# Attention-then-FFN kernel: token chunks of 112 partitions with the last 16 tokens in the first chunk, split loads, and small-tile matmuls collected into three bundles a batch

## The chip, the cores and the metric

One core of a Trainium2 chip runs the whole program. The metric is device time in microseconds (us) of one execution; three runs of the kernel before gave 705.81, 705.86 and 706.18, median 705.86.

## What is computed

```python
# q, k, v: (8 batches, 8 heads, 576 tokens, 64); phi: (8, 8, 576, 32), float32
a = exp(phi - max(phi, axis=2)); a = a / (sum(a, axis=2) + 1e-9)      # over the tokens
k_m = einsum('bhsm,bhsd->bhmd', a, k); v_m = einsum('bhsm,bhsd->bhmd', a, v)
scores = q @ k_m.T / 8
attn = softmax(scores, axis=-1)                                        # over 32 memories
x = (attn @ v_m) as (4608 tokens, 512)
h = x @ w_in                                                           # w_in: (512, 2048)
out = (h * erf(softplus(h))) @ w_out                                   # w_out: (2048, 512)
```

## The kernel before, in words

The kernel never forms `x`. For each batch it multiplies the 32 memories of each head of `v_m` into `w_in` once (`vw`, L675), so that the first FFN product of a hidden chunk of 128 is attention weights times `vw` (`ffn1`, L752, matmul L770). Matmuls of that stage and of the second FFN product (`ffn2`, L851, matmul L847) are made at float32 accuracy from three fp32r products of a high and a low part. Steps are numbered by (batch, hidden chunk): 16 chunks a batch, 128 steps in all. One step is two halves of `ffn1` (6 matmuls of 288 columns each into a bank of tag `ps`), softplus, erf and a product on ACT and DVE, and 12 matmuls of `ffn2` of an earlier step into four `pso` banks. The 64 tokens of a batch that are left over 4 x 128 go two batches at a time through `ffn2_rest` (L869, tile `psr`, one `ps` bank for its whole run).

**Small-tile work on PE.** Beside these full-array matmuls each batch needs: the sums over tokens that make `k_m` and `v_m` (`sums_and_turn`, L580, matmul L598; 128x32 tiles of the array), their turning by transposes (L629), the transposes that spread the maxima of phi (`phi_numbers`, L508, L515), two groups of score matmuls (`attention`, L700, through `of_heads`, L663, matmul L667, 64x32 tiles) and four groups of `vw` (also L667, 64x32 tiles, 512 columns; 256 columns in batch 0). The transposes use the whole 128x128 array. `together` (L546) makes operations that are to be issued in one run, of kind "small"; `bundle` (L948) and the list `PARTS` (L975 to 992) say at which step which of them go together. For batches 3 to 7 the work for batch b stands in four bundles, all during batch b-1: sums with `vw` 4, turn with phi_numbers of the next batch and `vw` 8, scores 2b with `vw` 12, scores 2b+1 with the first `vw` of batch b. In the last batch three `vw` bundles stand alone.

**Order.** The order on each engine is fixed when the program is built. `Plan` runs a list scheduler over all operations, with a rank for each (`at(step)`), a cost, an engine or two ways, and room in each pool (`room`, L306: four `ps` banks; 4 + 4 tiles of `at_hi` and `at_lo`; five `raw` tiles). L1016 to 1021 shift the ranks of eight operations and fix the engine of one. Each DMA is issued on SP (`load`, L388), at the start also on ACT (`queue`, L384). At the start of the program PE is filled with dummy matmuls (`fill`, L372).

**Loads.** Tokens lie on 116 partitions in five chunks; the host pads each chunk to 128 rows (`rows`, L1049). A `kv` load (`load_kv`, L412) moves 128 partitions x 5 chunks x 1 KB = 640 KB, of which 64 KB is padding rows; q of half a batch is one load of 576 KB into a `raw` tile (`load_q`, L418; into `wo` for batch 0).

Of the kernel before, what the change touches and what calls it, by code (L numbers as in the profile page):

```python
# [32 lines left out]
ROW = 116  # L33
# [214 lines left out]
def tile_memory_attention_then_erf_softplus_ffn(  # L248
# [29 lines left out]
    ROWS = [min(ROW, S - c * ROW) for c in range(NC)]  # L278
    assert NC == -(-S // ROW) and D < ROWS[-1] and H == 8
# [11 lines left out]
        for n, b, kw in (  # L291
# [4 lines left out]
            ("at", 4, {}),  # L296
# [9 lines left out]
    room = {"wo": NPR, "vw_hi": 2, "vw_lo": 2, "at_hi": 4, "at_lo": 4, "h": HB, "e": EB}  # L306
# [111 lines left out]
    def load_q(rank, u, tag="raw"):  # L418
        key = tile_(tag, "q", u, shape=[P, NP_, U], pool=tag)
        b, hf = divmod(u, 2)  # L420
        load(rank, P * NP_ * U * 4, [key], lambda: nc.sync.dma_start(
            out=get(key),
            in_=qT[b, hf].rearrange("r (p s) -> r p s", p=NP_)))


# [82 lines left out]
    def phi_numbers(rank, b):  # L508

        a, bias = ("phi", b), ("bias", b)  # L510
        ps = tile_("ps", "psa", "max", b, shape=[P, H * M], pool="ps")

        def turn():
            for g in range(NG):
                nc.tensor.transpose(  # L515
                    out=get(ps)[:, g * P : (g + 1) * P], in_=get(bias)[:, g], identity=ident
                )

        yield
        yield 2 * 108, [bias], [ps], [], turn  # L520
        op(DVE, on_dve(NC * H * M), rank, [a, ps], [a], lambda: nc.vector.tensor_tensor(  # L521
            out=get(a)[:ROW], in0=get(a)[:ROW],
            in1=get(ps)[:ROW].unsqueeze(1).to_broadcast([ROW, NC, H * M]), op=ALU.add))
        op(ACT, on_act(NC * H * M), rank, [a], [a], lambda: nc.scalar.activation(
            get(a)[:ROW], get(a)[:ROW], AF.Exp), kind="exp")

    def memories(rank, rank_2, b, parts):

        a = ("phi", b)
        phi_sums(rank, b)  # L530
        if b:
            together(rank, phi_numbers(rank, b))
        else:
            tile_("raw", *a, shape=[P, NC, H * M], pool="raw")
            n = NC - 1
            for g in range(NG):
                numbers_of(rank, b, g, range(n), tile_("ps", "psa", "a", g, shape=[P, n, P], pool="ps"), 0)
            last = tile_("ps", "psa", "a", NG, shape=[P, NG, P], pool="ps")
            for g in range(NG):
                numbers_of(rank, b, g, range(n, NC), last, g)  # L540
# [5 lines left out]
    def together(rank, *pieces):  # L546
# [5 lines left out]
        holds = [k for w in works for k in w[2] + w[3]]  # L552
        for n, (cost, _, writes, _, emit) in enumerate(works):
            x = op(PE, cost, rank + n * 1e-3, reads, writes, emit, kind="small",
                   holds=[] if n else holds)
            x.follows, before_it = before_it, x
        for x in pieces:
            next(x, None)

    def numbers_of(rank, b, g, cs, ps, at):  # L560

        t, a, n, ln = ("phiT", b, g), ("phi", b), len(cs), ROWS[cs[0]]

        def turn():
            for c in cs:
                nc.tensor.transpose(
                    out=get(ps)[:ln, at + c - cs[0], :], in_=get(t)[:, c * ROW : c * ROW + ln], identity=ident
                )
# [11 lines left out]
    def sums_and_turn(rank, b, part, rank_2=None):  # L580
# [5 lines left out]
        ps, t = ("psa", "kmvm", b, part), ("kvk", b, part)  # L586
        ps_2 = ("psa", "turn", b, part)
# [4 lines left out]
        def sums():  # L592
            for n, g in enumerate(gs):
                for c, ln in enumerate(ROWS):
                    for j in range(4):
# [3 lines left out]
                            out=get(ps)[M * j : M * (j + 1), n, :w],  # L599
# [8 lines left out]
        def first():  # L608
            tile_("ps", *ps, shape=[P, 4, P], pool="ps")
            tile_("dk", *t, shape=[P, 4, 2, D], pool="att")  # L610
            yield
            yield n_g * NC * 110 * n_x, [a] + kvs, [ps], [t], sums
            for n, g in enumerate(gs):
                rs = ("prs", b, g)

                def keep(f, n=n):
                    return lambda: f(
                        get(t)[:, n * n_x : (n + 1) * n_x],
                        get(ps)[:, n, : n_x * D].rearrange("p (x d) -> p x d", d=D).unsqueeze(2)
                        .to_broadcast([P, n_x, 2, D]))  # L620

                op(ACT, on_act(2 * n_x * D, True), rank, [ps, rs], [(t, n)],
# [40 lines left out]
    def of_heads(ps, w, x):  # L663
        for p in range(NP_):
            for par in range(2):
                rows = slice(par * D, (par + 1) * D)
                nc.tensor.matmul(  # L667
                    out=get(ps[par])[p * M : (p + 1) * M, :],
                    lhsT=w[rows, p, :],
                    rhs=x[rows, p, :],  # L670
# [4 lines left out]
    def vw(rank, b, k, n, exact):  # L675
# [3 lines left out]
        if k % 4 == 0:  # L679
            tile_("vw_hi", *hi, shape=[P, 2, 512], dtype=F32 if exact else F32R, pool="vw")  # L680
            if not exact:
# [5 lines left out]
               lambda: of_heads(ps, vm[b % 2], w_in_sb[i][:, :, cols]))  # L687
# [12 lines left out]
    def attention(rank, rank_2, u):  # L700
        b = u // 2
        s = tile_("sc", "sc", u)
        ps = heads(U, "sc", u)
        yield
        yield (4 * U / 2.4, [("km", b % 2), ("q", u)], ps, [s],
               lambda: of_heads(ps, km[b % 2], get(("q", u))))
# [7 lines left out]
        for g in range(NG):  # L714
            op(DVE, on_dve(U), rank, [ps[g]], [(s, g)], lambda g=g: nc.vector.transpose(
                out=get(s)[:, g, :], in_=get(ps[g])))
# [152 lines left out]
    def ffn2_rest(rank, b, first, n):  # L869
# [12 lines left out]
        op(PE, 3 * n * mm(DM, False), rank, reads + [o], [o], emit)  # L882
# [14 lines left out]
    def at(step):  # L897
        return 100 * step
# [13 lines left out]
    for n, name in enumerate(FIRST):  # L912
# [5 lines left out]
        elif name[:-1] == "q":  # L918
            load_q(rank, x, "wo")
# [33 lines left out]

    for b in range(1, B):
        o = NK * b
        n = o - 12 if b == 1 else o - {2: 18, 3: 26}.get(b, 34)
        for g in range(NG):
            when(n, load_phiT, at(n - 6 if b <= 2 else n - 3), b, g)
        n, n_3 = (n if b <= 3 else o - 28), n + 2
        when(n, load_phi, at(n - 5), b)  # L960
        n_2 = n if b <= 2 else o - 17
# [3 lines left out]
        if b > 2:  # L965
            when(n_3, phi_sums, at(n_3), b)
        else:
            if b == 1:
                when(n, memories, at(n), at(n + 3), b, TOGETHER)
            else:  # L970
                when(n, phi_sums, at(n), b)
        for x in range(2):
            n = o - 8 + 4 * x if b == 1 else o - 13
            when(n, load_q, at(n - 4 + 2 * x), 2 * b + x)
        PARTS = [(o - 8, [(attention, 2 * b)]), (o - 4, [(attention, 2 * b + 1), (vw, b, 0)])]  # L975
        if b > 1:
            m = o - (11 if b == 2 else 15)
            sums, turn = sums_and_turn(at(m), b, TOGETHER[0], at(o - 11))
            PARTS = [(m, [(sums,), (vw, b - 1, 8 if b == 2 else 4)])]
            if b == 2:  # L980
                PARTS = [(o - 15, [(phi_numbers, b), (vw, b - 1, 4)])] + PARTS
            later = [(phi_numbers, b + 1)] if b + 1 < B else []
            PARTS += [
                *([(o - 11, [(turn,)]), (o - 3, later)] if b == 2 else
                  [(o - 11, [(turn,)] + later + [(vw, b - 1, 8)])]),
                (o - 7, [(attention, 2 * b), (vw, b - 1, 12)]),
                (o - 4, [(attention, 2 * b + 1), (vw, b, 0)]),
            ]
        if b == B - 1:
            PARTS += [(o + 1, [(vw, b, 4)]), (o + 5, [(vw, b, 8)]), (o + 9, [(vw, b, 12)])]  # L990
        for n, fs in PARTS:
            when(n, bundle, at(n), fs)
# [93 lines left out]
```

## Time and profile before

| | us |
|---|---|
| median of three runs | 705.86 |
| the profiled execution, its own time | 706.31 |
| its span, first to last instruction | 704.5 |
| PE busy | 696.3 |
| ACT busy | 488.7 |
| DVE busy | 448.9 |
| POOL busy | 108.2 |

The profile has the busy time of each engine, the span in 40 slices, the chain of work that ended last, and groups of instructions by source line. Matmuls are pipelined, so what a matmul costs PE is read from the distance between starts, not from the duration of one. [...]

### The profile page before, as it was taken

What the parts mean: (1) busy time and instruction counts of PE and PEld (TensorE: products, weight loads), DVE (VectorE), ACT (ScalarE), POOL (GpSimd) and SP (SyncE); (2) the same over time, 40 slices, a digit from 0 to 9 for tenths busy, and PEclk for the clock granted to TensorE, in tenths of its full rate; (3) what the DMA queues carried; (4) which work ended last, traced back from release to release, by engine and by line L of the source; (5) the groups of instructions that cost most, each with busy time, mean ns of one, the idle gap of its engine ahead of it and who ended that gap; (6) DMA issues with size and microseconds to landing.
All of it is one profiled execution on the core that took longest, in us unless ns stands there. A gap on an engine that the chain in (4) does not pass through costs nothing.

```text
span 704.5 us, 12292 instructions
## 1 busy us (share of the span) xinstructions
PE 696.3 (99%) x4858; PEld 560.5 (80%) x4858; DVE 448.9 (64%) x774; ACT 488.7 (69%) x793; POOL 108.2 (15%) x262
## 2 busy tenths in 40 slices
PE   8999999999999999999999999999999999999997
PEld 4556588888888888888888788888888888888886
DVE  4999999468734686567734677546764348745530
ACT  4899989757855768787754867776665556776821
POOL 0032135112111111111201111101111011111110
PEclk9999999999999999999999999999999999999999
DMA  9999100712312115030132102311120100010002
GB/s 362 418 414 417 40 26 17 297 41 68 117 65 92 55 38 181 30 102 13 56 150 77 44 27 68 151 60 38 39 68 1 61 15 1 1 60 1 1 1 75
DMA packets 17833, 66.71 MB, mean 95 GB/s; under 512 B 2032, under 2 KB 2032, under 8 KB 17776
## 3 DMA queue, kind: packets, MB, share of 16 engines
q1 hardware_dynamic: 17408, 64.85, 24.8%
q10 hardware_dynamic: 368, 1.08, 0.4%
q8 instruction: 38, 0.62, 0.4%
q14 instruction: 19, 0.16, 0.1%
HBM read 56.49 MB, written 9.44 MB: 94 GB/s over the span
## 4 chain that ended last, share of the span: by engine, by line
PE 92%; DMA 4%; DVE 2%; ACT 1%; issue 0%; SPq 0%
PE pso L847 50%; PE psh L770 28%; PE psr L847 6%; PE psa L667 6%; PE psa L598 2%; DMA q<-qT 2%; DMA phiT<-phiT 2%; PE psa L629 0%; DVE w L441 0%; PE psa L515 0%; DVE phi L521 0%; DVE pmx L490 0%; ACT L810 0%; ACT e L805 0%; DVE sc L729 0%
## 5 line engine op out<-in xcount | busy, mean ns | idle before, releaser
L847 PE MATMUL pso<-wo,g_hi 128*128 128x512 f32 x960 | 300.0, 394 | 0.0
L847 PEld LDWEIGHTS pso<-wo,g_hi 128*128 128x128 f32 x960 | 172.2, 188 | 41.1 <-issue 12.6
L847 PE MATMUL pso<-wo,g_lo 128*128 128x512 f32 x480 | 188.2, 392 | 0.0
L788 ACT ACTIVATE h<-psh 128x288 f32<-128x288 f32 x176 | 71.6, 409 | 137.1 <-PE psh L770 136.7
L836 DVE TENSOR_TENSOR e<-e,h 128x576 f32<-128x576 f32 x120 | 88.6, 754 | 51.2 <-ACT e L810 51.1
L843 POOL CAST rest<-g_hi 128x64 fp32r<-128x64 f32 x120 | 55.0, 458 | 423.4 <-DVE g_hi L838 419.3
L838 DVE CAST g_hi<-e 128x576 fp32r<-128x576 f32 x120 | 53.9, 450 | 101.3 <-PE pso L847 96.7
L770 PE MATMUL psh<-at_hi,vw_hi 128*128 128x288 f32 x496 | 109.5, 302 | 0.0
L847 PEld LDWEIGHTS pso<-wo,g_lo 128*128 128x128 f32 x480 | 90.1, 188 | 20.6
L770 PE MATMUL psh<-at_lo,vw_hi 128*128 128x288 f32 x496 | 106.2, 296 | 0.0
L770 PE MATMUL psh<-at_hi,vw_lo 128*128 128x288 f32 x496 | 105.6, 294 | 0.0
L770 PEld LDWEIGHTS psh<-at_hi,vw_hi 128*128 128x128 f32 x496 | 85.7, 188 | 21.0 <-issue 3.7
L839 DVE TENSOR_TENSOR g_lo<-e,g_hi 128x576 fp32r<-128x576 f32 x120 | 92.3, 769 | 7.6 <-POOL rest L843 0.5
L805 ACT ACTIVATE e<-h 128x576 f32<-128x576 f32 x127 | 86.7, 685 | 3.4 <-DVE h L787 0.7
L810 ACT ACTIVATE e<-e 128x576 f32<-128x576 f32 x128 | 79.8, 675 | 0.4
L770 PEld LDWEIGHTS psh<-at_hi,vw_lo 128*128 128x128 f32 x496 | 79.9, 188 | 0.0
L770 PEld LDWEIGHTS psh<-at_lo,vw_hi 128*128 128x128 f32 x496 | 79.3, 188 | 0.0
L843 POOL CAST rest<-g_lo 128x64 fp32r<-128x64 f32 x120 | 40.7, 340 | 98.8 <-DVE g_lo L839 95.9
L847 PE MATMUL psr<-wo,rest 128*128 128x512 f32 x192 | 49.1, 391 | 0.0
L365 ACT ACTIVATE vw_hi<-psa 128x512 fp32r<-128x512 f32 (+1 forms) x68 | 34.8, 555 | 18.7 <-PE psa L667 18.6
L367 DVE TENSOR_TENSOR vw_lo<-psa,vw_hi 128x512 fp32r<-128x512 f32 (+1 forms) x68 | 40.6, 636 | 9.8 <-ACT vw_hi L365 9.5
L847 PEld LDWEIGHTS psr<-wo,rest 128*128 128x128 f32 x192 | 36.0, 188 | 8.7 <-POOL rest L843 0.8
(81 smaller groups left out, 650.4 us busy)
## 6 DMA issues: line engine op xcount, KB each, us to landing
kv<-kv SPq DMA_DIRECT2D x31, 640.0 KB, 8.1
q<-qT SPq DMA_DIRECT2D x16, 576.0 KB, 5.4
out<-ot SPq DMA_DIRECT2D x32, 256.0 KB, 2.0
w<-w_in SPq DMA_DIRECT2D x8, 1023.8 KB, 15.6
w<-w_out SPq DMA_DIRECT2D x8, 1023.8 KB, 14.8
phi<-phi SPq DMA_DIRECT2D x7, 640.0 KB, 7.1
phiT<-phiT SPq DMA_DIRECT2D x15, 288.0 KB, 3.8
out<-ot SPq DMA_DIRECT2D x7, 128.0 KB, 2.3
```

Of the source, the lines that this page charges most:

```text
L365: lambda: nc.scalar.activation(get_hi(), get_src(), AF.Identity))
L367: lambda: nc.vector.tensor_tensor(out=get_lo(), in0=get_src(), in1=get_hi().bitcast(F32), op=ALU.subtract))
L667: nc.tensor.matmul(out=get(ps[par])[p * M : (p + 1) * M, :], lhsT=w[rows, p, :], rhs=x[rows, p, :], start=True, stop=True,)
L770: nc.tensor.matmul(out=get(ps)[:, :U], lhsT=x[:, g, k % 4 * P : (k % 4 + 1) * P], rhs=y[:, g, :], start=(n + g == 0), stop=(n == len(parts ...
L788: other={ACT: (on_act(U, True), lambda: nc.scalar.activation(keep(), get(ps), AF.Identity))})
L805: last[:] = [op(ACT, on_act(S), rank, [("h", i)], [e], lambda: nc.scalar.activation(get(e), get(("h", i)), AF.Softplus), kind="softplus", ...
L810: last[:] = [op(ACT, on_act(S), rank, [e], [e], lambda: nc.scalar.activation(get(e), get(e), AF.Erf), kind="erf", edge=edge, after=last)]
L836: op(DVE, on_dve(S), rank, [e, h], [e], lambda: nc.vector.tensor_tensor(out=get(e), in0=get(e), in1=get(h), op=ALU.mult))
L838: op(DVE, on_dve(S, 1), rank, [e], [hi], lambda: nc.vector.tensor_copy(out=get(hi), in_=get(e)))
L839: op(DVE, on_dve(S), rank, [e, hi], [lo], lambda: nc.vector.tensor_tensor(out=get(lo), in0=get(e), in1=get(hi).bitcast(F32), op=ALU.subtract))
L843: lambda x=x, y=y: nc.gpsimd.tensor_copy(out=rest[:, k, x, cols], in_=get(y)[:, NT * P :]))
L847: nc.tensor.matmul(out=o, lhsT=y, rhs=z, start=(start and n == 0), stop=(stop and n == len(parts) - 1))
```

## The change

1. **Layout.** `ROW` is 112. The chunks are 128, 112, 112, 112, 112 tokens: the first chunk holds tokens 0 to 111 on partitions 0 to 111 and the last 16 tokens on partitions 112 to 127. The host lays out `kv`, `phi` and `phiT` so. The phi operations cover 128 partitions instead of 116.
2. **Loads.** A `kv` load is two transfers: 112 partitions x 5 KB, and 16 partitions x 1 KB. From batch 1 on, q of half a batch is two transfers of half the size into tiles of the pool `at`, no longer `raw`. `at_hi` and `at_lo` share eight tiles `at` with them.
3. **Bundles.** `PARTS` is rewritten. In batches 2 to 6 it has three bundles: at step 1 scores 2b+2 with `vw` 4; at step 7.5 `vw` 8 with `vw` 12; at step 12 the sums of batch b+2, scores 2b+3 and the first `vw` of batch b+1. The last batch has two. `phi_numbers` and the turn stand alone (`alone`, no longer of kind "small"). From batch 3 on the sums are written into columns 288 to 415 of the two banks of the scores they are bundled with, and not into a bank of their own.
4. **Smaller edits.** The transposes of `phi_numbers` also wait for the phi load. `ffn2_rest` comes two operations a step from step 2, not one a step from step 0, and its first follows the last bundle made. Ten ranks and four engine choices replace the list at L1016.

The core of the diff:

```diff
-ROW = 116
+ROW = 112
-    ROWS = [min(ROW, S - c * ROW) for c in range(NC)]
+    ROWS = [P] + [ROW] * (NC - 1)
-    room = {"wo": NPR, "vw_hi": 2, "vw_lo": 2, "at_hi": 4, "at_lo": 4, "h": HB, "e": EB}
+    room = {"wo": NPR, "vw_hi": 2, "vw_lo": 2, "at": 8, "h": HB, "e": EB}
...
-        load(rank, P * NC * 4 * D * 4, [key], lambda: queue(b, g if x == 0 else 0).dma_start(out=get(key), in_=src))
+        by = queue(b, g if x == 0 else 0)
+        load(rank, ROW * NC * 4 * D * 4, [(key, 0)], lambda: by.dma_start(out=get(key)[:ROW], in_=src[:ROW]))
+        load(rank, (P - ROW) * 4 * D * 4, [(key, 1)],
+             lambda: by.dma_start(out=get(key)[ROW:, 0], in_=src[ROW:, 0]))
...
+        for x in range(2):
+            key = tile_("at", "q", u, x, shape=[P, 2, U], pool="at")
+            load(rank, P * 2 * U * 4, [key], lambda x=x, key=key: nc.sync.dma_start(
+                out=get(key), in_=src[:, 2 * x : 2 * x + 2]))
...
-        yield 2 * 108, [bias], [ps], [], turn
+        yield 2 * 108, [bias, a], [ps], [], turn
...
+        banks = [ps] * n_g if into is None else [("psa", "sc", into, n) for n in range(n_g)]
...
+    def alone(rank, x):
+        together(rank, x, kind=None)
...
-            PARTS = [(m, [(sums,), (vw, b - 1, 8 if b == 2 else 4)])]
...
-                  [(o - 11, [(turn,)] + later + [(vw, b - 1, 8)])]),
-                (o - 7, [(attention, 2 * b), (vw, b - 1, 12)]),
-                (o - 4, [(attention, 2 * b + 1), (vw, b, 0)]),
...
-            PARTS += [(o + 1, [(vw, b, 4)]), (o + 5, [(vw, b, 8)]), (o + 9, [(vw, b, 12)])]
+            PARTS += [
+                (o + 1, [(phi_numbers, 2), (vw, 1, 4)]),
+                (o + 5, [(sums[2],), (vw, 1, 8)]),
+                (o + 5, [(turn[2],)]),
+                (o + 9, [(attention, 4), (vw, 1, 12)]),
+            ]
+        elif b < B - 1:
+            PARTS += [(o + 1, [(attention, 2 * b + 2), (vw, b, 4)]), (o + 7.5, [(vw, b, 8), (vw, b, 12)])]
+        else:
+            PARTS += [(o + 1, [(vw, b, 4)]), (o + 7.5, [(vw, b, 8), (vw, b, 12)])]
+        if b + 2 < B:
+            n = o + 10 if b == 1 else o + 8
+            when(n, lambda n=n, b=b: alone(at(n), phi_numbers(at(n), b + 2)))
+            n = o + 14
+            when(n, lambda n=n, b=b: alone(at(n), turn[b + 2]))
+        if b + 1 < B:
+            PARTS += [(o + 12, with_sums(b + 2) + [
+                (attention, 2 * b + 3, 2 * D * (b + 2 < B)), (vw, b + 1, 0)])]
...
-            n = (b + 1) * NK + k // 2 if b < B - 1 else max(second[NS - NK + k + 1] + 1, NS)
+            n = (b + 1) * NK + 2 + k // 4 if b < B - 1 else max(second[NS - NK + k + 1] + 1, NS)
...
-        90: 380, 128: 213, 179: 257, 222: 139, 250: -309, 251: -309, 252: -309, 253: -309,
+        67: -130, 95: -149, 108: -209, 134: 157, 213: 238, 259: -312, 260: -312, 296: 307,
+        303: 463, 597: 396,
-    for n, e in {105: ACT}.items():
+    for n, e in {109: DVE, 136: ACT, 326: DVE, 500: DVE}.items():
```

## Rows read from the trace of the kernel before

**Rows 1.** The page: busy time, share of the span and instructions of each engine; and by line, the shares of the chain that ended last.

```profile
PE 696.3 (99%) x4858; PEld 560.5 (80%) x4858; DVE 448.9 (64%) x774; ACT 488.7 (69%) x793; POOL 108.2 (15%) x262
PE pso L847 50%; PE psh L770 28%; PE psr L847 6%; PE psa L667 6%; PE psa L598 2%; DMA q<-qT 2%; DMA phiT<-phiT 2%; PE psa L629 0%; DVE w L441 0%; PE psa L515 0%; DVE phi L521 0%; DVE pmx L490 0%; ACT L810 0%; ACT e L805 0%; DVE sc L729 0%
```

**Rows 2.** Windows of the span: stretch, its length, busy us of PE, weight loads, DVE, ACT and POOL (instructions), granted clock, DMA share, GB/s.

```profile
4.00:20.00 16.00, 14.58 (x242) 7.91 (x240) 9.92 (x22) 6.44 (x14) 0.00 (x0) 1.00 1.02 422
20.00:40.00 20.00, 19.46 (x128) 12.66 (x122) 19.74 (x29) 18.48 (x34) 0.56 (x2) 1.00 1.01 415
40.00:70.00 30.00, 29.71 (x247) 18.10 (x246) 29.39 (x43) 29.31 (x49) 9.72 (x13) 1.00 1.02 417
70.00:100.00 30.00, 30.00 (x176) 20.69 (x175) 30.00 (x52) 26.20 (x40) 8.75 (x10) 1.00 0.13 45
100.00:650.00 550.00, 549.63 (x3832) 457.60 (x3831) 342.94 (x606) 385.58 (x625) 82.86 (x214) 1.00 0.19 65
```

**Rows 3.** PE in order of time around one bundle of scores and `vw` (start us, us from first start to last end, line, tiles, shape, count).

```profile
401.50 0.62 PE L847 MATMUL pso<-wo,g_hi 128*128 128x512 f32 x2
401.96 0.40 PE L847 MATMUL pso<-wo,g_lo 128*128 128x512 f32 x1
402.28 0.72 PE L667 MATMUL psa<-q,km 64*32 64x288 f32 x16
402.79 1.06 PE L667 MATMUL psa<-w_in,vm 64*32 64x512 f32 x16
403.79 0.74 PE L847 MATMUL pso<-wo,g_hi 128*128 128x512 f32 x2
404.37 0.39 PE L847 MATMUL pso<-wo,g_lo 128*128 128x512 f32 x1
```

**Rows 4.** PE in order of time: the other small-tile operations of the same batch, then the three of the last batch; between them stand only full-array matmuls.

```profile
348.10 2.40 PE L598 MATMUL psa<-kv,phi 116*32 116x128 f32 x80
350.43 1.09 PE L667 MATMUL psa<-w_in,vm 64*32 64x512 f32 x16
...
393.69 0.60 PE L629 MATMUL psa<-ident,kvk 128*128 128x128 f32 x4
394.12 0.38 PE L515 MATMUL psa<-ident,bias 128*128 128x128 f32 x2
394.44 1.09 PE L667 MATMUL psa<-w_in,vm 64*32 64x512 f32 x16
...
421.36 0.72 PE L667 MATMUL psa<-q,km 64*32 64x288 f32 x16
421.87 1.06 PE L667 MATMUL psa<-w_in,vm 64*32 64x512 f32 x16
...
603.34 1.09 PE L667 MATMUL psa<-w_in,vm 64*32 64x512 f32 x16
...
622.69 1.09 PE L667 MATMUL psa<-w_in,vm 64*32 64x512 f32 x16
...
641.24 1.09 PE L667 MATMUL psa<-w_in,vm 64*32 64x512 f32 x16
```

**Rows 5.** Windows of line L667 alone, 100 to 650 us: PE busy us and matmul records, then the weight loads.

```profile
100.00:650.00 550.00, 35.22 (x624) 8.57 (x624) 1.00 0.19 65
```

**Rows 6.** PE in order of time: a `vw` group of 256 columns early in the program, with what follows it.

```profile
56.71 0.66 PE L667 MATMUL psa<-w_in,vm 64*32 64x256 f32 x16
57.30 0.53 PE L770 MATMUL psh<-at_hi,vw_hi 128*128 128x288 f32 x2
```

**Rows 7.** PE in order of time: transposes followed by full-array matmuls.

```profile
129.16 0.66 PE L629 MATMUL psa<-ident,kvk 128*128 128x128 f32 x4
129.57 0.70 PE L847 MATMUL pso<-wo,g_hi 128*128 128x512 f32 x2
130.11 0.40 PE L847 MATMUL pso<-wo,g_lo 128*128 128x512 f32 x1
```

**Rows 8.** The chain that ended last, its first 30 us in order of time (start us, us, what).

```profile
0.74 3.88 DMA phiT<-phiT
...
4.64 12.99 DMA q<-qT
...
17.76 0.82 PE psa L667 x16
18.58 0.83 DVE sc L715 x2
...
25.29 1.14 DVE w_in L465
```

**Rows 9.** DVE in order of time: the transposes of the second half batch's scores, with the idle time before them.

```profile
18.56 0.85 DVE L715 STREAM_TRANSPOSE sc<-psa 128x288 f32<-128x288 f32 x2 [0.86 <-PE psa L667]
```

**Rows 10.** SP's queue in order of time: the DMA issues of the first 20 us (three of them).

```profile
1.19 0.42 SPq L416 DMA_DIRECT2D kv<-kv  x1
2.60 1.05 SPq L416 DMA_DIRECT2D kv<-kv  x2
4.64 0.33 SPq L421 DMA_DIRECT2D q<-qT  x1
```

**Rows 11.** The page's DMA issues: tile, queue, count, KB each, median us from issue to landing.

```profile
kv<-kv SPq DMA_DIRECT2D x31, 640.0 KB, 8.1
...
phi<-phi SPq DMA_DIRECT2D x7, 640.0 KB, 7.1
...
out<-ot SPq DMA_DIRECT2D x7, 128.0 KB, 2.3
```

**Rows 12.** What ACT and DVE did right after the bundle of rows 3 (start us, us, line, operation, tiles, shapes, count, idle before).

```profile
403.95 1.09 ACT L365 ACTIVATE vw_hi<-psa 128x512 fp32r<-128x512 f32 x2 [0.91 <-PE psa L667]
403.09 0.85 DVE L715 STREAM_TRANSPOSE sc<-psa 128x288 f32<-128x288 f32 x2 [1.62 <-PE psa L667]
403.97 0.75 DVE L718 TENSOR_REDUCE smx<-sc 128x18 f32<-128x576 f32 x1
404.64 1.28 DVE L367 TENSOR_TENSOR vw_lo<-psa,vw_hi 128x512 fp32r<-128x512 f32 x2
```

**Rows 13.** Two of PE's weight loads' waits, whole run: who waited for whom, us in total, times, longest us.

```profile
PEld psa L667 <- issue: 5.9, 23, 0.4
PEld psr L847 <- POOL rest L843: 0.8, 1, 0.8
```

More of the change, by code (lines that the diff above doesn't have):

```diff
@@ L277, in tile_memory_attention_then_erf_softplus_ffn @@
     NC = phi.shape[2]
-    ROWS = [min(ROW, S - c * ROW) for c in range(NC)]
-    assert NC == -(-S // ROW) and D < ROWS[-1] and H == 8
+    ROWS = [P] + [ROW] * (NC - 1)
+    AT = [sum(ROWS[:c]) for c in range(NC)]
+    assert sum(ROWS) == S and D < ROW and H == 8
     RAW = 5
@@ L415, in load_kv, with load_q, q_keys, q_of @@
         src = kv[b - 1, 2 * g + x] if b else kv_0[x, g]
-        load(rank, P * NC * 4 * D * 4, [key], lambda: queue(b, g if x == 0 else 0).dma_start(out=get(key), in_=src))
-    def load_q(rank, u, tag="raw"):
-        key = tile_(tag, "q", u, shape=[P, NP_, U], pool=tag)
-        b, hf = divmod(u, 2)
-        load(rank, P * NP_ * U * 4, [key], lambda: nc.sync.dma_start(
-            out=get(key),
-            in_=qT[b, hf].rearrange("r (p s) -> r p s", p=NP_)))
+        by = queue(b, g if x == 0 else 0)
+        load(rank, ROW * NC * 4 * D * 4, [(key, 0)], lambda: by.dma_start(out=get(key)[:ROW], in_=src[:ROW]))
+        load(rank, (P - ROW) * 4 * D * 4, [(key, 1)],
+             lambda: by.dma_start(out=get(key)[ROW:, 0], in_=src[ROW:, 0]))
+    def load_q(rank, u):
+        b, hf = divmod(u, 2)
+        src = qT[b, hf].rearrange("r (p s) -> r p s", p=NP_)
+        if u < 2:
+            key = tile_("wo", "q", u, shape=[P, NP_, U], pool="wo")
+            load(rank, P * NP_ * U * 4, [key], lambda: nc.sync.dma_start(out=get(key), in_=src))
+            return
+        for x in range(2):
+            key = tile_("at", "q", u, x, shape=[P, 2, U], pool="at")
+            load(rank, P * 2 * U * 4, [key], lambda x=x, key=key: nc.sync.dma_start(
+                out=get(key), in_=src[:, 2 * x : 2 * x + 2]))
+    def q_keys(u):
+        return [("q", u)] if u < 2 else [("q", u, x) for x in range(2)]
+    def q_of(u, rows, p):
+        return get(("q", u))[rows, p] if u < 2 else get(("q", u, p // 2))[rows, p % 2]
     wo, wf, raw_of = {}, {}, {}
@@ L536, in memories @@
             for g in range(NG):
-                numbers_of(rank, b, g, range(n), tile_("ps", "psa", "a", g, shape=[P, n, P], pool="ps"), 0)
-            last = tile_("ps", "psa", "a", NG, shape=[P, NG, P], pool="ps")
+                numbers_of(rank, b, g, range(1, NC), tile_("ps", "psa", "a", g, shape=[P, n, P], pool="ps"), 0)
+            whole = tile_("ps", "psa", "a", NG, shape=[P, NG, P], pool="ps")
             for g in range(NG):
-                numbers_of(rank, b, g, range(n, NC), last, g)
+                numbers_of(rank, b, g, range(1), whole, g)
         for turn_n, part in enumerate(parts):
@@ L544, in memories, with together @@
             together(rank_2 + turn_n * 0.01, second)
-    def together(rank, *pieces):
+    bundles = []
+    def together(rank, *pieces, kind="small"):
         for x in pieces:
@@ L551, in together @@
         reads = [k for w in works for k in w[1]]
-        holds = [k for w in works for k in w[2] + w[3]]
+        holds = [k[0] if isinstance(k[0], tuple) else k for w in works for k in w[2] + w[3]]
         for n, (cost, _, writes, _, emit) in enumerate(works):
-            x = op(PE, cost, rank + n * 1e-3, reads, writes, emit, kind="small",
+            x = op(PE, cost, rank + n * 1e-3, reads, writes, emit, kind=kind,
                    holds=[] if n else holds)
             x.follows, before_it = before_it, x
+        if kind == "small":
+            bundles.append(x)
         for x in pieces:
@@ L578, in numbers_of, with sums_and_turn @@
                lambda y, x: nc.scalar.activation(y, x, AF.Identity)))})
-    def sums_and_turn(rank, b, part, rank_2=None):
+    def sums_and_turn(rank, b, part, rank_2=None, into=None):
         rank_2 = rank if rank_2 is None else rank_2
@@ L586, in sums_and_turn, with sums_of @@
         ps, t = ("psa", "kmvm", b, part), ("kvk", b, part)
+        banks = [ps] * n_g if into is None else [("psa", "sc", into, n) for n in range(n_g)]
+        def sums_of(n):
+            if into is None:
+                return get(ps)[:, n, : n_x * D]
+            return get(banks[n])[:, U : U + n_x * D]
         ps_2 = ("psa", "turn", b, part)
@@ L598, in sums @@
                         nc.tensor.matmul(
-                            out=get(ps)[M * j : M * (j + 1), n, :w],
+                            out=sums_of(n)[M * j : M * (j + 1)],
                             lhsT=get(a)[:ln, c, h * M : (h + 1) * M],
@@ L608, in first @@
         def first():
-            tile_("ps", *ps, shape=[P, 4, P], pool="ps")
+            if into is None:
+                tile_("ps", *ps, shape=[P, 4, P], pool="ps")
             tile_("dk", *t, shape=[P, 4, 2, D], pool="att")
             yield
-            yield n_g * NC * 110 * n_x, [a] + kvs, [ps], [t], sums
+            yield n_g * NC * 110 * n_x, [a] + kvs, [ps] if into is None else [(k, "sums") for k in banks], [t], sums
             for n, g in enumerate(gs):
@@ L618, in keep @@
                         get(t)[:, n * n_x : (n + 1) * n_x],
-                        get(ps)[:, n, : n_x * D].rearrange("p (x d) -> p x d", d=D).unsqueeze(2)
+                        sums_of(n).rearrange("p (x d) -> p x d", d=D).unsqueeze(2)
                         .to_broadcast([P, n_x, 2, D]))
-                op(ACT, on_act(2 * n_x * D, True), rank, [ps, rs], [(t, n)],
+                op(ACT, on_act(2 * n_x * D, True), rank, [ps if into is None else (banks[n], "sums"), rs], [(t, n)],
                    keep(lambda y, x, rs=rs: nc.scalar.activation(y, x, AF.Identity, scale=get(rs))),
@@ L667, in of_heads @@
                 nc.tensor.matmul(
-                    out=get(ps[par])[p * M : (p + 1) * M, :],
+                    out=get(ps[par])[p * M : (p + 1) * M, :n],
                     lhsT=w[rows, p, :],
-                    rhs=x[rows, p, :],
+                    rhs=x_of(rows, p),
                     start=True,
@@ L697, in vw, with attention @@
                       lambda par=par: get(ps[par]), True)
-    def attention(rank, rank_2, u):
+    def attention(rank, rank_2, u, more=0):
         b = u // 2
         s = tile_("sc", "sc", u)
-        ps = heads(U, "sc", u)
+        ps = heads(U + more, "sc", u)
         yield
-        yield (4 * U / 2.4, [("km", b % 2), ("q", u)], ps, [s],
-               lambda: of_heads(ps, km[b % 2], get(("q", u))))
+        yield (4 * U / 2.4, [("km", b % 2)] + q_keys(u), [(k, "sc") for k in ps], [s],
+               lambda: of_heads(ps, km[b % 2], lambda rows, p: q_of(u, rows, p), U))
         def view():
@@ L714, in attention @@
         for g in range(NG):
-            op(DVE, on_dve(U), rank, [ps[g]], [(s, g)], lambda g=g: nc.vector.transpose(
-                out=get(s)[:, g, :], in_=get(ps[g])))
+            op(DVE, on_dve(U), rank, [(ps[g], "sc")], [(s, g)], lambda g=g: nc.vector.transpose(
+                out=get(s)[:, g, :], in_=get(ps[g])[:, :U]))
         mx, sm, rs = (tile_(n, n, u) for n in ("smx", "ssm", "srs"))
@@ L881, in ffn2_rest @@
         reads += [wo[k // 2] for k in range(first, first + n)]
-        op(PE, 3 * n * mm(DM, False), rank, reads + [o], [o], emit)
+        op(PE, 3 * n * mm(DM, False), rank, reads + [o], [o], emit,
+           after=bundles[-1:] if first == 0 else ())
         if first + n == NK:
@@ L918, in tile_memory_attention_then_erf_softplus_ffn @@
         elif name[:-1] == "q":
-            load_q(rank, x, "wo")
+            load_q(rank, x)
         else:
@@ L983, in tile_memory_attention_then_erf_softplus_ffn, with with_sums @@
+    def with_sums(b):
+        return [(sums[b],)] if b < B else []
+    PARTS = [(NK - 8, [(attention, 2)]), (NK - 4, [(attention, 3), (vw, 1, 0)])]
+    for b in range(1, B):
+        o = NK * b
+        if b == 1:
             PARTS += [
-                *([(o - 11, [(turn,)]), (o - 3, later)] if b == 2 else
-                  [(o - 11, [(turn,)] + later + [(vw, b - 1, 8)])]),
-                (o - 7, [(attention, 2 * b), (vw, b - 1, 12)]),
-                (o - 4, [(attention, 2 * b + 1), (vw, b, 0)]),
-            ]
@@ L993, in tile_memory_attention_then_erf_softplus_ffn @@
+        if b + 2 < B:
[6 more added lines that the diff above has]
+                (attention, 2 * b + 3, 2 * D * (b + 2 < B)), (vw, b + 1, 0)])]
+    for n, fs in PARTS:
+        when(int(n), bundle, at(n), fs)
     for b in range(1, B, 2):
         for k in range(0, NK, 2):
-            n = (b + 1) * NK + k // 2 if b < B - 1 else max(second[NS - NK + k + 1] + 1, NS)
+            n = (b + 1) * NK + 2 + k // 4 if b < B - 1 else max(second[NS - NK + k + 1] + 1, NS)
@@ L1051, in rows, with turned @@
         *lead, s, e = x.shape
-        n = -(-s // ROW)
+        n = s // ROW
         y = np.zeros((*lead, n, 128, e), x.dtype)
-        for c in range(n):
-            z = x[..., c * ROW : (c + 1) * ROW, :]
-            y[..., c, : z.shape[-2], :] = z
+        y[..., :ROW, :] = x[..., : n * ROW, :].reshape(*lead, n, ROW, e)
+        y[..., 0, ROW:, :] = x[..., n * ROW :, :]
         return np.moveaxis(y, -2, -3)
+    def turned(x):
+        n = x.shape[-1] // ROW * ROW
+        return np.concatenate([x[..., :ROW], x[..., n:], x[..., ROW:n]], -1)
     kv = np.stack([k, v])
@@ L1066 @@
         "phi": rows(phi.transpose(0, 2, 1, 3).reshape(B, S, H * M)),
-        "phiT": phi.transpose(0, 1, 3, 2).reshape(B, H * M, S),
+        "phiT": turned(phi.transpose(0, 1, 3, 2).reshape(B, H * M, S)),
         "w_in": moe_w_in.reshape(H // 2, 2 * D, DFF // 256, 256).transpose(1, 2, 0, 3)
```

50 lines of the change are left out of this document (21 added, 29 removed).

## The prediction

> **What bounds the kernel now.** First the page: PE is busy for 99% of the span and the chain that ended last is PE for nine tenths; its DMA is q's and phiT's loads, most of it at the start [rows 1, 8]. Then the windows, which part the span in two [rows 2]. From 4 to 70 us the 16 DMA engines are full (share 1.02, 415 to 422 GB/s), and from 20 to 100 us DVE is full too (19.74 of 20, 29.39 of 30, 30.00 of 30 us). From 100 to 650 us PE is busy 549.63 of 550 us, DVE and ACT for 343 and 386, DMA for a fifth. So there only PE time counts: a load or an evacuation that gets cheaper gives nothing, a PE stall that vanishes gives all of itself. Busy time hides those stalls, since a matmul's duration overlaps its neighbours; the timeline's starts show them. Last the chain of the first 30 us [rows 8]: a phiT load, then q's load until 17.63, then PE, DVE and ACT in turn.
>
> About 0.2% (1.4 us) is what a measurement of this kernel can tell from no change.
>
> **Visits to small tiles: how many.** I call a visit a run of small-tile matmuls between full-array ones. Line 667 has 624 records from 100 to 650 us [rows 5], 16 to a group: 39 groups, 12 of scores (two for each of batches 2 to 7) and 27 of `vw`. Each visit holds exactly one `vw` group, as the batch at 348 to 422 us and the last one show [rows 4], so there are 27. The new list makes 4 in batch 1, 3 in each of batches 2 to 6 and 2 in the last: 21. Six go, one a batch. (The change is described as three for five; before it the rows show four a batch, beside which no separate visit for transposes exists.)
>
> **Visits: what one costs.** Full-array matmuls of 512 columns start every 0.23 us (0.46 for two). Into the visit it took 402.28 - 401.96 = 0.32: 0.09 more. After it the first pair took 404.37 - 403.79 = 0.58: 0.12 more. In between, a `vw` group of 512 columns that is followed by full-array work takes 1.00 us [rows 3] and one of 256 columns 0.59 [rows 6]; 256 columns cost 0.41, so 0.18 of either is not columns. How much of that goes when another small group follows no row shows: between none and 0.18. I take 0.12, nearer the upper end, since scores before `vw` take 0.51 for 288 columns [rows 3], where 0.41 x 288/256 = 0.46 is columns: 0.05 of overhead is left, not 0.18. A visit costs 0.21 to 0.39, I take 0.33. Six: **-1.98 us** (-1.26 to -2.34).
>
> [...]
>
> Sums, in 128x32 tiles, now meet scores in place of `vw`; both are 64x32, so the 2.33 us from the sums' start to the next group [rows 4] stay. Columns, rows and counts of all matmuls stay.
>
> **Transposes alone.** Ten runs of transposes, two for each of batches 3 to 7, leave the visits for full-array work. Four take 0.43 us [rows 4]; four with the next pair took 130.11 - 129.16 = 0.95 [rows 7], against 0.43 + 0.46, and that pair came out of a visit as well. So 0 to 0.06 each; I take 0.01: **+0.1 us** (0 to +0.6).
>
> **The start.** Four kv loads come ahead of q's second half, each 64 KB smaller once the padding is gone: 262 KB at 422 GB/s is 0.62 us. The chain runs through exactly this landing [rows 8], and DVE sat idle 0.86 us for the scores behind it [rows 9]; after that it is full until 100 us. So what DVE starts earlier, the first `ffn1` does too, until PE becomes the bound near 43 us. The gain lies between nothing, if another input of DVE's next work is as late, and 0.62: **-0.5 us**, near the upper end because the idle time is longer than the shift. The ranks shift other work on DVE here as well; one decode operation moved out of or into the way is 1.14 us [rows 8], either sign. I take 0 for it and keep 1.14 for the range.
>
> **What I cost at nothing, and what hides it.** The 32 second pieces of kv and 14 of q are 46 more issues on SP at 0.33 us [rows 10]; SP only issues, mostly waiting for a buffer, and kv is taken for 8.1 us to landing [rows 11], several steps before its use. If a load ceased to be early, PE would pay 0.33 in that batch. At the start three more issues on SP and one on ACT push the others back by 0.4 each; DMA is full then, so the data waits and not the issue. With q out of `raw`, kv no longer waits for a buffer that q holds. The transposes of phi's maxima now wait for phi; behind them on PE stands `ffn1`. Phi lands in 7.1 us [rows 11] and its rank lies nine steps ahead of theirs; without that cover PE would stop for the rest of 7.1 us. The leftover product puts 12 matmuls where 6 were, two steps earlier; PE waited for POOL's casts there once, 0.8 us [rows 13], so three batches could pay 2.4; I take 0. ACT and DVE have 0.3 to 0.4 of their time free, and their work stays.
>
> For the split of the loads, the rows say that transfers follow each other without a gap at DMA share 1.02 [rows 2], so that a 16 KB piece costs its bytes, 0.04 us. [...]
>
> **Sum.** -1.98 + 0.1 - 0.5 = -2.38. The profiled execution took 706.31 (span 704.5 and 1.8 around it), so 703.93; it lay 0.45 above the median of the runs, so 703.5.
>
> **Rivals.**
> *The start gives nothing.* The scores of the first half batch hang on phi and not on k, and v's sums or the first `w_in` might come just as late. For it: DVE is full from 20 us. Against: the 0.86 us. Then -1.88: 704.0. Chance 20%.
>
> *PSUM banks (the slower side).* `vw` with `vw` (six times) and sums with scores and `vw` (five) take all four `ps` banks, and the next `ffn1` needs one. ACT takes 0.55 and DVE 0.64 for one half of a `vw` group, and DVE did a 0.75 us reduction in between [rows 12]. Until then PE has only `ffn2`, 12 matmuls or 2.75 us, and these need a `g` that is ready. For it: a scores bank went free after 0.43 of DVE alone; now the first bank needs ACT and DVE, or, in the bundle with sums, two readers. [...] Break-even is 2.38/11 = 0.22 us a bundle; from 0.34 the kernel is slower by over 0.2%. At 0.5, well under one evacuation of 1.19: +5.5, 709.0. Chance 6%. At 0.2: 705.7; visits that the scheduler parts again would end near 705.5. Together 13%.
>
> *Small transfers hold the queue.* If each of the four 16 KB pieces ahead of q cost what the smallest store takes from issue to landing, 2.3 us [rows 11], q would land 9.2 - 0.62 = 8.6 us later: 706.31 - 1.88 + 8.6 - 0.45 = 712.6. Against: the full DMA share. Chance 2%. [...]
>
> *More than forecast.* A decode operation out of the way at the start gives 1.14 more, 702.4; twelve visits gone in place of six, 701.5. Chance 13%.
>
> **Chances.** The forecast has 46% (its own range 702.9 to 704.4). It, four fifths of the first rival and the last are faster by over 0.2%, under 704.45: 74%. Within 0.2%: 18%, the small waits and the rest of the first rival. Slower: 8%. The range 702.0 to 705.9 takes in the forecast, the start without gain, most of the small waits and the start's better end; it leaves out the two slow rivals and twelve visits.
>
> **What would show it.** Right: 21 visits after 100 us; `vw` to `vw` in a bundle in about 0.9 us from start to start; full-array starts 0.23 us apart before and after the transposes; q's second half landing near 17.0 us and DVE's wait of 0.86 us down to 0.3; from 100 us to the last matmul about 1.9 us less. Wrong: a wait of `ffn1` behind a bundle, q landing no earlier, 27 visits, or PE waiting for POOL or phi.

## The result and the profile after

The changed kernel took 710.82 us (median of six runs, 710.11 to 711.93) beside 706.18 for the kernel before in the same session: ratio 1.0068, 95% interval 1.0057 to 1.0079. It is slower by 4.6 us where 2.4 us of gain was forecast. The profiled execution took 710.78, its span is 709.0.

First the five stretches of [rows 2] in the kernel after (same columns):

```profile
4.00:20.00 16.00, 12.51 (x222) 7.21 (x220) 8.27 (x17) 5.91 (x12) 0.00 (x0) 1.00 1.02 356
20.00:40.00 20.00, 19.99 (x131) 12.95 (x124) 19.55 (x30) 17.13 (x30) 0.00 (x0) 1.00 1.02 372
40.00:70.00 30.00, 28.65 (x236) 17.11 (x235) 25.86 (x42) 26.02 (x45) 5.43 (x11) 1.00 1.02 367
70.00:100.00 30.00, 30.00 (x184) 19.42 (x183) 30.00 (x45) 25.98 (x42) 13.06 (x13) 1.00 0.43 132
100.00:650.00 550.00, 549.09 (x3829) 458.19 (x3828) 347.91 (x615) 393.00 (x633) 84.43 (x214) 1.00 0.21 63
```

The DMA engines are as full as before (1.02 to 70 us) and move 10 to 16% less a second: 356 where 422 stood, 372 for 415, 367 for 417. The loads last into the next stretch (share 0.43, before 0.13). That points at packets that take longer: in the first 70 us those of 5,120 bytes take 272 ns here and 200 before (both measured below). The page's list of DMA issues [rows 11] agrees, smaller load and longer landing:

```profile
kv<-kv SPq DMA_DIRECT2D x31, 560.0 KB, 9.4
```

The chain of work that ended last, pieces of its first 60 us, to be set against [rows 8] (start us, us, what):

```profile
1.18 7.70 DMA kv<-kv
...
9.25 10.13 DMA q<-qT
...
21.96 16.19 DMA kv<-kv
...
38.58 12.23 DMA w<-w_in
...
52.01 1.35 DVE w L455
```

q's second half lands at 19.38 us (9.25 + 10.13) where it landed at 17.63, though 262 KB less lie ahead of it. After it the chain goes through four pieces on PE and then not on through DVE and ACT but back into loads, until 50.81. Three of PE's waits for other engines and loads (for whom, us in total, times, longest) follow; the first and the last say the same, and DVE's wait of 0.86 us for the second half's scores [rows 9] became 2.25:

```profile
PE psa L623 <- DMA kv<-kv: 2.6, 3, 1.1
...
PE psh L796 <- DVE vw_lo L368: 0.8, 1, 0.8
PE psa L693 <- DMA q<-qT: 0.5, 1, 0.5
```

```profile
20.32 0.48 DVE L741 STREAM_TRANSPOSE sc<-psa 128x288 f32<-128x288 f32 x1 [2.25 <-PE psa L693]
```

The middle entry of PE's waits belongs to a second loss, at 150 to 155 us. DVE in order of time there, then PE:

```profile
150.84 0.75 DVE L504 TENSOR_REDUCE pmx<-phiT 128x1 f32<-128x576 f32 x1 [1.49 <-DMA phiT<-phiT]
...
152.86 0.75 DVE L504 TENSOR_REDUCE pmx<-phiT 128x1 f32<-128x576 f32 x1 [0.51 <-DMA phiT<-phiT]
153.53 1.28 DVE L368 TENSOR_TENSOR vw_lo<-psa,vw_hi 128x512 fp32r<-128x512 f32 x2
```

```profile
153.03 0.43 PE L796 MATMUL psh<-at_hi,vw_lo 128*128 128x288 f32 x2
154.26 0.54 PE L796 MATMUL psh<-at_hi,vw_hi 128*128 128x288 f32 x2 [0.80 <-DVE vw_lo L368]
```

phiT's two loads stand on SP behind batch 3's phi and four kv loads. They are late, DVE waits 2.0 us for them, `vw_lo` stands behind them on DVE, and the next `ffn1` on PE waits 0.80 us for it (taken to be for the PSUM bank that `vw_lo` reads).

What was forecast for the visits did happen. PE in order of time around `vw` 8 with `vw` 12, which answers to [rows 3], and around four transposes alone [rows 7]:

```profile
227.33 0.39 PE L873 MATMUL pso<-wo,g_lo 128*128 128x512 f32 x1
227.65 1.95 PE L693 MATMUL psa<-w_in,vm 64*32 64x512 f32 x32
229.52 0.73 PE L873 MATMUL pso<-wo,g_hi 128*128 128x512 f32 x2
230.09 0.40 PE L873 MATMUL pso<-wo,g_lo 128*128 128x512 f32 x1
...
265.66 0.60 PE L655 MATMUL psa<-ident,kvk 128*128 128x128 f32 x4
266.02 0.70 PE L873 MATMUL pso<-wo,g_hi 128*128 128x512 f32 x2
266.56 0.40 PE L873 MATMUL pso<-wo,g_lo 128*128 128x512 f32 x1
```

Two `vw` groups take 229.52 - 227.65 = 1.87. The second is followed by full-array work and takes 1.00 [rows 3], so the first takes 0.87: 0.13 saved. Entry is 0.32 - 0.23 = 0.09 and the first pair after is 0.57 - 0.46 = 0.11 late. A visit that goes is worth 0.33, as forecast. Transposes with the next pair take 0.90, against 0.43 + 0.46.

### The profile page after: what moved, and what is told of

Its sections match the earlier page's. It is cut to its first block, busy times and chain, and to the rows that moved or that the text cites. A ratio compares the mean times of both kernels' runs of the same rounds, so it can differ in the third digit from the quotient of the medians.

```text
span 709.0 us, 12370 instructions
## 1 busy us (share of the span) xinstructions
PE 697.5 (98%) x4860; PEld 562.4 (79%) x4860; DVE 449.7 (63%) x775; ACT 492.3 (69%) x796; POOL 109.8 (15%) x262
## 3 DMA queue, kind: packets, MB, share of 16 engines
q10 hardware_dynamic: 384, 1.02, 0.5%
## 4 chain that ended last, share of the span: by engine, by line
PE 89%; DMA 9%; DVE 0%; ACT 0%; issue 0%; SPq 0%; ACTq 0%
PE pso L873 49%; PE psh L796 26%; PE psr L873 6%; PE psa L693 5%; DMA kv<-kv 4%; PE psa L623 2%; DMA w<-w_in 2%; DMA q<-qT 1%; DMA out<-ot 1%; DMA phiT<-phiT 0%; PE psa L655 0%; DVE w L455 0%; DVE w_in L479 0%; ACT w L452 0%; PE psa L529 0%
## 5 line engine op out<-in xcount | busy, mean ns | idle before, releaser
L796 PEld LDWEIGHTS psh<-at_hi,vw_hi 128*128 128x128 f32 x496 | 87.2, 188 | 18.5 <-issue 3.1
L869 POOL CAST rest<-g_lo 128x64 fp32r<-128x64 f32 x120 | 42.5, 355 | 97.3 <-DVE g_lo L865 94.3
L813 DVE COPY h<-psh 128x288 f32<-128x288 f32 x79 | 35.1, 449 | 15.7 <-PE psh L796 15.2
```

The costliest lines, as they stand in the source:

```text
L796: nc.tensor.matmul(out=get(ps)[:, :U], lhsT=x[:, g, k % 4 * P : (k % 4 + 1) * P], rhs=y[:, g, :], start=(n + g == 0), stop=(n == len(parts ...
L813: lambda: nc.vector.tensor_copy(out=keep(), in_=get(ps)),
L869: lambda x=x, y=y: nc.gpsimd.tensor_copy(out=rest[:, k, x, cols], in_=get(y)[:, NT * P :]))
```

## The experiments

Theory T: a transfer of 112 partitions moves its packets more slowly than one of 128, so that the smaller load takes longer; this and not the bundles costs the time. Rivals on record: the number of transfers, the 16-partition piece, the layout's arithmetic, the count of rows an engine gets.

The nine kernels differ from the one that they are edited from only by the edits shown or named. In the first four PE, DVE, ACT and POOL keep that kernel's order of work. Each set of runs had the kernel before beside it, at 705.89 to 706.06. A packet here is one record in the trace's list of DMA packets: the four kv loads ahead of q's second half show one of 5,120 bytes for each partition, 512 in the kernel before and 448 in the changed one. Packet times below are means over the trace's packet records that start before 70 us, grouped by size; the 5,120-byte group also holds phi's rows, from loads of 128 partitions, so in the runs with a split this mean is not that of the kv loads alone.

**The load whole again.**

```diff
-        load(rank, ROW * NC * 4 * D * 4, [(key, 0)], lambda: by.dma_start(out=get(key)[:ROW], in_=src[:ROW]))
-        load(rank, (P - ROW) * 4 * D * 4, [(key, 1)],
-             lambda: by.dma_start(out=get(key)[ROW:, 0], in_=src[ROW:, 0]))
+        load(rank, ROW * NC * 4 * D * 4, [(key, 0)], lambda: by.dma_start(out=get(key), in_=src))
+        load(rank, (P - ROW) * 4 * D * 4, [(key, 1)], lambda: None)
```

> The changed kernel with each kv load as one transfer of 128 partitions x 5 KB again (640 KB, padding and all), and no second piece; the order on PE, DVE, ACT and POOL is the changed kernel's, instruction by instruction. Theory T: the transfers of 112 partitions move slowly, their 5 KB packets taking 276 to 303 ns where those of 128-partition loads took 196 to 202; this delays the start and, later, phiT of batch 3, behind which DVE and then PE stop at 151 to 154 us. By T packets here take 196 to 202 ns, q of the second half batch lands near 17.6 us (19.4 in the changed kernel), the stop at 151 to 154 us is gone, and the time is 706.18 less six visits of 0.34: 704.2 (703.6 to 705.0). Rival B: the new bundles or ranks hold up the start and PSUM; then it stays at 709 to 711. Rival S (two transfers a load use up the eight semaphores that DMAs in flight share, so that later loads are issued late) gives 704.2 as well; the runs with two pieces tell it from T.

705.20 us, ratio to before 0.9991 (0.9982 to 0.9999). Packets of 5,120 bytes take 200 ns; they took 272 in the changed kernel and 200 in the kernel before. The windows are back at the old rate:

```profile
4.00:20.00 16.00, 14.42 (x242) 7.91 (x240) 9.77 (x22) 6.43 (x14) 0.00 (x0) 1.00 1.02 422
20.00:40.00 20.00, 19.98 (x127) 12.79 (x121) 19.87 (x30) 18.41 (x34) 0.77 (x2) 1.00 1.02 415
```

Since PE's order is the same in both, one can subtract the start of each `ffn2` matmul here from that of the same matmul in the changed kernel: the changed kernel is 1.8 us later at 41 us, 3.9 at 57, 4.4 from 71 us on, 4.6 at 148 and 6.2 from 178 us on. So the start costs 4.4, and the late phiT of batch 3 another 1.65 (here DVE does not wait for it). At 556 to 571 us 1.3 come back, because this kernel stalls there on its own:

```profile
557.50 1.15 ACT L916 ACTIVATE ot<-pso 128x512 f32<-128x512 f32 x2 [1.32 <-DMA out<-ot]
```

```profile
558.15 0.74 PE L872 MATMUL pso<-wo,g_hi 128*128 128x512 f32 x2 [0.57 <-ACT ot L916]
...
563.15 0.72 PE L872 MATMUL pso<-wo,g_hi 128*128 128x512 f32 x2 [0.36 <-ACT ot L916]
```

The mechanism holds; the time is 1 us above the 704.2 that I expected and outside its range, and that stall is as large.

**Two pieces of 128 partitions.**

```diff
+        load(rank, ROW * NC * 4 * D * 4, [(key, 0)], lambda: by.dma_start(out=get(key)[:, 1:], in_=src[:, 1:]))
+        load(rank, (P - ROW) * 4 * D * 4, [(key, 1)], lambda: by.dma_start(out=get(key)[:, 0], in_=src[:, 0]))
```

> The changed kernel with each kv load as two transfers of 128 partitions each: chunks 1 to 4 (4 KB a partition) and chunk 0 (1 KB), 640 KB together; as many transfers, semaphores and issues as in the changed kernel, and its order. Theory T: 4 KB packets near 160 ns (1.6 times 98 for 2.5 KB, at 26 GB/s an engine), time 704.2 to 705.2. Rival S: still 709 to 711, since the number of transfers is the same.

705.54 us, 0.9993 (0.9984 to 1.0002), 0.3 above the range expected. 4,096-byte packets take 164 ns, 1,024-byte ones 47. As many transfers as in the change, and next to nothing lost: their number is not the cause. It does delay the issues: q's second half is issued at 7.93 us here, at 9.25 in the changed kernel and at 4.64 before [rows 10]. But it lands here at 17.91, 0.28 after the 17.63 of before, though issued 3.29 later: with the DMA engines full (share 1.03 from 4 to 20 us) the later issue cost little here.

**112 partitions, without a piece of 16.**

```diff
+        load(rank, ROW * NC * 4 * D * 4, [(key, 0)],
+             lambda: by.dma_start(out=get(key)[:ROW, 1:], in_=src[:ROW, 1:]))
+        load(rank, (P - ROW) * 4 * D * 4, [(key, 1)], lambda: by.dma_start(out=get(key)[:, 0], in_=src[:, 0]))
```

> The changed kernel with each kv load as 112 partitions x 4 KB (chunks 1 to 4) and 128 partitions x 1 KB (chunk 0): the same 576 KB without padding, two transfers, but no piece of 16 partitions. Theory T: the 4 KB packets of the 112 partitions take 215 to 240 ns in place of some 157, time 708.5 to 711. If the 16-partition pieces were what slows the queue (rival P): 4 KB packets near 160 ns and 704 to 705.

711.03 us, 1.0070 (1.0055 to 1.0085). From the run before only 16 partitions of the 4-KB piece are gone: its packets take 241 ns where they took 164. The 16-partition piece is not needed for the loss.

**The split alone, with the bundles of before.** The kernel before, with the change's layout and both its transfers in one operation.

```diff
+        def both():
+            by.dma_start(out=get(key)[:ROW], in_=src[:ROW])
+            by.dma_start(out=get(key)[ROW:, 0], in_=src[ROW:, 0])
```

> The kernel before with the new layout and the split kv loads (112 partitions x 5 KB and 16 x 1 KB) alone: old bundles, ranks, pools and whole q loads, order on PE, DVE and POOL as before. Theory T: packets of 270 to 300 ns, q of the second half batch near 19.5 us, the first 100 us longer by 3 to 5: 709.5 to 711. Rival B: nothing but the saved bytes, 705.5 to 706.3. Rival S: 708 to 711, with packets at 200 ns.

714.50 us, 1.0117 (1.0103 to 1.0130); 5,120-byte packets at 277 ns. Sign and cause are as expected, the size is above the range. PE's order is that of the layout alone (next run), so the starts can be subtracted: this run is 1.9 us later at 19.5 us, 3.1 at 24, 2.8 at 34, 3.9 at 60, 6.3 at 111 and 8.1 at 153. Most of what goes beyond the changed kernel is thus lost from 60 to 111 us, and there the chain that ended last lies in a load of `w` from 62.3 to 78.4 us. In this run the granted TensorE clock is 0.91 from 20 to 40 us, where the changed kernel had 1.00. By the starts that costs 1.2 us at most. Its first two windows:

```profile
4.00:20.00 16.00, 13.23 (x222) 7.44 (x220) 8.54 (x18) 5.87 (x12) 0.00 (x0) 1.00 1.03 351
20.00:40.00 20.00, 20.00 (x128) 12.91 (x120) 19.15 (x28) 16.53 (x30) 0.00 (x0) 0.91 1.02 394
```

**The layout alone, whole loads, the bundles of before.** Edit: as the last one, with `load_kv` left as before.

> The kernel before with the layout of the change alone (chunks of 112, the last 16 tokens in the first chunk's partitions 112 to 127), its five bundles a batch, its ranks and its loads of one 640-KB transfer of 128 partitions. Theory T (the layout and its arithmetic cost nothing, only the 112-partition load does): 705.6 to 706.3 us, 5,120-byte packets at 199 ns, q of the second half batch landing near 17.6 us. Set beside the whole load with the new bundles (705.2 us) it then gives what the six visits are worth, 0.7 us of the 1.98 forecast. Rival L, the layout costs time of its own that the bundles paid for in that run: 706.5 to 707.5.

706.11 us, 1.0000 (0.9990 to 1.0009). The layout and its arithmetic cost nothing that these runs can tell.

**Two halves of 64 and 48 partitions.**

```diff
+            by.dma_start(out=get(key)[:64], in_=src[:64])
+            by.dma_start(out=get(key)[64:ROW], in_=src[64:ROW])
```

> The changed kernel with its 112-partition load cut into two transfers, partitions 0 to 63 and 64 to 111, 5 KB a partition; the 16-partition piece as it was. The bytes are the same, the partitions of a transfer fewer. [...] Rival C, what slows it is that 112 rows leave some engine an odd share (7 rows): rows of 4 and 3 an engine come at about 200 ns, and the time is 705.2 to 707. Rival B, packets of 5,120 bytes from this layout are slow however they are cut: 272 ns stays, and 710.5 to 711.5.

717.77 us, 1.0159 (1.0141 to 1.0178). 5,120-byte packets take 354 ns, 1.8 times those of a whole load, and the first window falls to 251 GB/s at full engines. So it is not the odd share of 7 rows an engine, by which they were to come at 200 ns:

```profile
4.00:20.00 16.00, 11.76 (x126) 6.81 (x124) 5.86 (x15) 5.19 (x11) 0.00 (x0) 0.89 1.02 251
```

**Same sizes, other partitions.** Two kernels, edited from the changed one, with the whole load in four transfers each (64 partitions x 4 KB, the same x 1 KB, two pieces of 32 x 5 KB); only which partitions they write differs. Each was timed twice. The diff is from the first of them to the second.

```diff
-            by.dma_start(out=get(key)[0:64, :4], in_=src[0:64, :4])
-            by.dma_start(out=get(key)[0:64, 4], in_=src[0:64, 4])
-            by.dma_start(out=get(key)[64:96], in_=src[64:96])
+            by.dma_start(out=get(key)[32:96, :4], in_=src[32:96, :4])
+            by.dma_start(out=get(key)[32:96, 4], in_=src[32:96, 4])
+            by.dma_start(out=get(key)[0:32], in_=src[0:32])
             by.dma_start(out=get(key)[96:128], in_=src[96:128])
```

> The changed kernel with each 640-KB load cut into four transfers: partitions 0 to 63 x 4 KB, partitions 0 to 63 x 1 KB, partitions 64 to 95 x 5 KB, partitions 96 to 127 x 5 KB. The number to read is the mean packet of the 64-partition 4-KB piece; with 128 partitions it was 163 ns, with 112 it was 240. [...] Rival C (how many partitions or rows an engine decides, not which): the same packet as in the run with partitions 32 to 95, whatever it is.

> As the run before it, with partitions 32 to 95 for the two 64-partition pieces, and 0 to 31 and 96 to 127 for the 5-KB pieces: the same sizes, counts and order of transfers, only other partitions. [...] Rival C: equal packets and times within 1 us.

| partitions of the 4-KB piece | packet, mean (median) ns | kernel, us |
|---|---|---|
| 128 | 164 (161) | 705.54 |
| 0 to 111 | 241 (245) | 711.03 |
| 0 to 63 | 299 (294) | 726.42 |
| 32 to 95 | 207 (165) | 717.79 |

The first two rows are of kernels above, with two transfers a load. From partition 32 the median packet is about as fast as in a transfer of 128 (165 and 161 ns), from partition 0 it takes 1.8 times as long (294), with the same number of partitions, bytes and transfers. So in these two runs, at equal number, it was decisive which partitions the transfers write. The mean of 207 lies well above its median of 165; the 32-partition pieces are slow in both runs (5,120-byte packets 295 ns here, 351 in the run from partition 0), and whether they hold up the others is not shown. The two kernels differ by 8.6 us, their times by at most 4.0 each.

**An output tile moved.** The whole-load kernel, with one remainder product's output in the other buffer.

```diff
-        final = o[1] >= B - 2 if o[0] == "psr" else o[1] == B - 1
+        final = o[1] >= B - 4 if o[0] == "psr" else o[1] == B - 1
```

> The changed kernel with whole 640-KB loads (705.2 us in its own runs), and the remainder rows' output tile (psr into ot) of the batch pair that is stored near 552 us in the other output buffer, so that two output tiles do not queue for the same two buffers within 0.5 us there; the hand order then puts that product some us later. In the whole-load run ACT waited 1.32 us there for a store that landed 4.3 us after its issue instead of 2.0 to 2.4, behind a 16-KB code fetch of 0.96 us, and PE 0.57 and 0.36 us behind ACT. Theory T2, this collision is what most of the missing part of the six visits' 1.98 us went to: 704.0 to 704.8 us, no wait of ACT for an out store near 550 to 565 us, and 0.7 to 1.2 us less than the whole load. Rival V, the visits are worth no more than the 0.7 us seen (what the profile shows saved at each is paid elsewhere in every run): 705.0 to 705.5, with or without that wait.

704.64 us, 0.9982 (0.9973 to 0.9991). Against their own runs of before the whole load gained 0.69 and this one 1.37: 0.7 more, the lower end of what was expected. I expected no wait of ACT for a store there; it still waits once (1.67 us, for a store that landed after 3.1), but the profile has no wait of PE from 100 to 650 us. That the collision took half of the visits' gain in the whole-load run is thereby likely, not shown: the edit also moved that product among its neighbours. Why the store was slow in the whole-load run is argued from one row, too: a code fetch of 16 KB (DMA queue q8, kind "instruction") stood on a DMA engine at the same time. Of that run's queues from 555 to 557.6 us, 2.3% of 16 engines for 2.6 us is 0.96 us on one:

```profile
q8 instruction: 1, 0.02, 2.3%
```

## Why the prediction was wrong

**The step that failed: the start, "-0.5 us".** I priced the smaller load by its bytes at 422 GB/s. All rows behind that rate are loads of 128 partitions [rows 2, 11]; that one of 112 runs at the same rate was assumed, and no row showed it. Measured, its packets are slower. By the trace's records, all packet time until q's landing, shared over 16 engines, is 15.9 us before and 17.9 in the changed kernel. The four kv loads ahead of q took 6.35 of it before (512 packets at 198 ns) and take 7.27 (448 at 260), so the smaller loads cost 0.9 us more. Their 1,024-byte packets add 0.2, and the two q loads, 220 ns a packet instead of 179, add 0.7. The sum of 1.8 is what q's landing slipped (19.38 - 17.63). The loads hold the chain until 51 us. Near 101 us the same `ffn2` matmul starts 4.4 us later than in the kernel before; with whole loads it starts at the same time. In place of -0.5 stands +4.4.

What the two runs of the same sizes show is that, at equal sizes and counts, the partitions written set the packet's time: 165 ns (median) with partitions 32 to 95, 294 with 0 to 63. Why the load of 112 takes longer than a whole one (241 ns against 164 for 4,096 bytes) stays open: no run here shows it.

**"What I cost at nothing: kv is taken early."** This failed too, for one batch. I priced a load that ceased to be early at 0.33 us; phiT of batch 3, behind the slow kv pieces, cost 1.65. With whole loads, or two pieces of 128 partitions, this loss is absent.

**The rivals.** *Small transfers hold the queue* had the sign and the place, q's landing, but the wrong piece: the four 16-KB pieces took 0.2 us of each engine's time ahead of q, not 9.2, and with a 128-KB piece in their place the time is the same (711.03 against 710.82). The large piece was the slow one. *PSUM banks* did not decide: the one wait of `ffn1` behind a bundle hangs on the late phiT and is gone with whole loads. *The start gives nothing* is nearest to what whole loads do. *More than forecast* has no row for it. In the chances, 46 + 16 + 13 make 75% for faster where 74 is stated, and 13 + 4 make 17% for no change where 18 is.

**Right.** Of the forecast signs, `vw` to `vw` took 0.87 ("about 0.9"), transposes alone nothing, and 432 records of `vw` from 100 us on are still 27 groups, in 21 visits. Six visits at 0.33 are 1.98. From 100 to 650 us the starts of PE's matmuls, beyond what the same matmuls take undisturbed, lose 1.7 to 1.8 us less in the kernel with the moved tile than in the kernel before (how much each loses hangs on what is called undisturbed, the difference hardly). In time that kernel stands 1.4 below before, the one with whole loads 0.7. So the visits' term was right as PE time, and between 0.7 and 1.4 of it came out; that the difference lies in which store meets which is argued, not shown.

**The balance.** The last matmul of the moved-tile kernel starts at 698.3 us, that of the kernel before at 699.9: -1.6. With the two losses, -1.6 + 4.4 + 1.65 = +4.5; measured +4.6. The changed kernel has no stall at its stores as the whole-load kernel had, hence the moved-tile kernel here.

## What to carry to other kernels

Price a DMA by the rate of rows of its own shape, partitions above all; if there is none, bound it with a loss too. Padding that fills 128 partitions can be cheaper than its removal: here 640 KB land in 8.1 us (median) and 560 in 9.4. When DMA's share stays full and its GB/s fall (here 1.02, and 356 where 422 stood), ask what became slow about a packet before asking what was issued too late.

## What the runs showed of the hardware

A 4,096-byte packet took 161 ns (median) with 128 partitions written, 165 with partitions 32 to 95, 245 with 0 to 111 and 294 with 0 to 63. In the first 70 us packets of other loads took longer too: `w`'s of 8,190 bytes a mean of 330 ns in the changed kernel and 315 before, q's of 4,608 bytes 220 and 181. Whether the slow transfers hold them up is not shown.

The granted TensorE clock was 0.91 from 20 to 40 us with the split alone and with 112 and 128 partitions, after 16 us in which PE was busy for 13.23 and 13.18. In the changed kernel, where it had been busy for 12.51, the clock stayed at 1.00. So late loads did not lower it in each run, and what does is not shown.
